# Attention and a gated MLP: the exponentials turned on VectorE in 32x32 blocks, the values as plain fp32 in 32x64 tiles

## The chip, the cores and the metric

One core of one Trainium2 chip runs the whole program. The metric is the device time of an execution in microseconds, the median of several runs.

## What is computed

Eight batches of eight heads, 576 positions, 64 values a head, all in fp32. Rotary attention is followed by an MLP with a spatial gate:

```python
def rotate(x):
    x1, x2 = (x[..., :half], x[..., half:])
    return np.concatenate([x1 * cos - x2 * sin, x1 * sin + x2 * cos], axis=-1)
q_rot, k_rot = (rotate(q), rotate(k))
scores = scale * np.matmul(q_rot, k_rot.transpose(0, 1, 3, 2))
scores = scores - np.max(scores, axis=-1, keepdims=True)
attn = np.exp(scores)
attn = attn / (np.sum(attn, axis=-1, keepdims=True) + 1e-09)
x = np.matmul(attn, v)          # then all heads side by side: (8, 576, 512)
h = np.maximum(x @ w_in, 0.0)   # 512 to 1024
u, v = (h[..., :d_ff // 2], h[..., d_ff // 2:])
v_n = (v - mean(v)) / sqrt(var(v) + 1e-06)
gated = u * (w_spatial @ v_n + b_spatial)
out = gated @ w_out
```

The weights of the MLP come as float64 and are decoded on the chip from their two 32-bit words.

## The kernel before

The unit of attention is a pair of heads; there are 32 pairs, four to a batch. A batch's MLP needs the four pairs of its batch, so it runs in among the attention of the next batch; the last batch's MLP runs alone.

Precision is kept by splitting each fp32 operand into a high and a low part of type fp32r and adding the products high by high, high by low and low by high. A matmul of fp32r is one weight load and one pass; a matmul of plain fp32 is two loads and two passes.

**Preparing a pair** (`prepare`). q and k are loaded transposed, each with a copy whose halves are swapped (two blocks of 576 columns in `st`). GpSimd multiplies both blocks with the tables `tabs` (L452) and adds them (L456); ScalarE and VectorE make the high and low parts; nine transfers on SP's queue stack them into `qs`, `ks` and `qz`, so that high and low parts of a head lie in the two halves of the partitions. Pair 0 alone (`prepare_whole`) keeps plain fp32.

**Scores** (`scores`). Nine chunks of 128 queries to a pair (five of them per head, the two heads' last 64 queries together). A chunk takes four matmuls of 288 columns (six for the joint one, L590; plain fp32 for pair 0, L600), then VectorE takes the maximum (L614) and ScalarE the exponential with its sum (L616). Two buffers `sc` of PSUM hold scores.

**Values** (`values`, pairs 4 to 31). TensorE transposes the exponentials in blocks of 128x128 (L633, 42 a pair), ScalarE copies the result as its high part (L644), VectorE subtracts to make the low part (L357), and TensorE multiplies both with the split V (L657); VectorE adds the two halves of the result (L672). Pairs 0 to 3 (`values_plain`) do the same without a split: transposes (L693), one copy (L700, L702), plain fp32 matmuls into the two 64-column tiles of the array, one per head (L731).

**Normalising** (`normalise`). The inverse sums are turned on VectorE (L765), written to DRAM and read back spread over the partitions (`rt`, `rb`); GpSimd multiplies (L769).

**MLP** (`mlp`). Per batch 360 matmuls in four stages: `pa` (L804, 512 columns), `pb` (L827), `pc` (L845), `pd` (L863), 288 columns each.

**The order** is written out before the program is built: `Program.run` is a planner that plays the instructions through with a cost for each, takes on every engine the ready one with the smallest key, and so fixes each engine's list. Keys are worked out from constants at the top (20 a pair, 80 a batch). Buffers are slots of pools (`SLOTS`); an instruction that needs one waits until it is free. Idle time of TensorE in the first 100 us is filled with matmuls on zeros (`warm`, L937). All loads and stacking transfers go on SP's queue.

Of the kernel before, what the change touches and what calls it, by code (L numbers as in the profile page):

```python
# [9 lines left out]
F32 = mybir.dt.float32  # L10
# [22 lines left out]
TO_PE = 105  # L33
SLOTS = {
    "stage": 3, "lk": 1, "vraw": 2, "vs": 2, "e2": 4, "e1": 2, "eh": 7, "rb": 1, "x32": 1, "xg": 7, "m": 4,
    "small": 3, "nmx": 3, "rt": 2, "sc": 2, "pv": 1, "pm": 3,
}
PSUM = {"sc": 1024, "pv": 512, "pm": 512}
MOE_START, MOE_LENGTH = 92.26, 81.46
DEC_V = [25.09, 132.15, 53.7, 5.9]  # L40
DEC_S = [56.31, 101.35, 34.39]
DEC_U = [50.38, 88.1, 14.23, 96.01]
DEC_ON = 5.18
DEC_O = [146.33, 201.67, 143.69, 195.96]

CHUNKS = [
# [3 lines left out]
]  # L50
CW = 3 * P

PLAIN = 4

WHOLE = 1
Q0 = 3 * TW
CHUNKS2 = [
    ([(0, 0), (1, 0), (0, 1), (1, 1), (0, 2), (1, 2)], [(0, P, 0, 0, 384)]),
    ([(0, 3), (1, 3), (0, 4)], [(0, P, 0, 384, 192)]),
]  # L60
S_AT2 = [[3.49, 4.95, -15.25, -11.82, -19.9, 2.65], [13.02, 24.28, 17.64]]
KT_STEP2 = [2.28, 0.35]
VALUES_AT2 = [-5.73, 46.17]
EARLY = 82.72
STEAL = 87.67
WARM_FROM, WARM_FULL, WARM_TO, WARM_NS, WARM_AFTER, WARM_COLS = 2500, 44958.22, 100000, 170, -0.15, 384
PATIENT = (DVE, ACT, POOL)
UNTIL = -56.22
LATE_LOAD = 2200
S_AT = [-0.24, 4.67, 2.11]  # L70
KT_STEP = 1.19
K_MAX, K_EXP, K_T, K_HI, K_LO, K_AV, K_HALF, K_ADD = 3.66, 16.17, 8.38, -7.48, 1.67, 4.25, 6.99, 12.36
K_LOAD, K_ROPE, K_SUM, K_HIQ, K_LOQ, K_LOK, K_STACK, K_STACK2, K_V, K_VLO = 27, 8, 8, 9, 9, 11, 30, 8, -2, -9
NORM = [-11.45, 57.29, 34.19, 6.63, 21.14]
FIRST = 6
PREP = [30.19, 35.32, -8.17, -24.92, 16.24, 1.9, 50.58, 22.5, 37.15, -9.46]
PREP_E = [54.12, 16.7, 11.17, -20.62, -5.02, 16.96, 39.13, 32.7, -16.4, -6.16]
PREP_AT = [4.76, 4.93, -9.37, 11.39, 24.89, 30.25]
PLAIN_E = [1.95, 2.05, -3.82, 3.33, 11.36]
PLAIN_AT = [-10.96, 10.02, -2.27, -27.43]  # L80
NORM_E = [38.01, -1.87, 12.98, 16.78, -11.57]
MOE0 = [87.11, 88.14]
K_NORM, K_RELU, K_GATE, K_GHI, K_GLO, K_OB, K_OUT = 28.57, -7.71, 10.98, 19.59, 15.51, -9.41, -27.84


def pe_ns(n, m=P):
    return max(m * 5 // 6 + 3, n * 11 // 24)
# [25 lines left out]
class Op:  # L113
    def __init__(self, costs, key, f, new, port, late):
        self.costs, self.key, self.f, self.new, self.port = costs, key, f, new, port
        self.eng, self.late = None, late
        self.waits, self.after, self.bufs = 0, [], []
        self.unknown, self.due = 0, 0


class Program:
# [5 lines left out]
    def op(self, eng, ns, key, f, r=(), w=(), new=(), port=False, late=0):  # L127
        return self.either({eng: ns}, key, lambda e: f(), r, w, new, port, late)

# [22 lines left out]
    def run(self, make, warm):  # L152
# [28 lines left out]
        idle = 0  # L181
        events.append((WARM_FROM, n, "wake", None))
# [3 lines left out]
        while events:  # L186
            now = events[0][0]
            while events and events[0][0] == now:
# [14 lines left out]
                else:  # L203
# [6 lines left out]
                    for a in o.after:  # L210
                        a.waits -= 1
                        if not a.waits:
                            late = TO_PE if PE in a.costs and o.eng != PE else 0
                            heapq.heappush(events, (now + late, n, "ready", a))
                            n += 1
            for e in LATENCY:
                if busy[e]:
                    continue
                passed, chosen = [], None
                while ready[e] and not chosen:  # L220
                    item = heapq.heappop(ready[e])
                    if item[2].eng:
                        continue
# [5 lines left out]
                    else:  # L229
                        passed.append(item)  # L230
                if chosen and e in PATIENT:
                    soon[e] = {a for a in soon[e] if not a.eng and a.due > now}
                    if any(a.key < min(chosen.key, UNTIL) and a.due < now + chosen.costs[e] * 0.5 for a in soon[e]):
# [7 lines left out]
                if e == PE and not chosen and max(WARM_FROM, idle + (WARM_AFTER if now > WARM_FULL else 0)) <= now < WARM_TO and (free["pv"] or free["pm"]):  # L241
                    chosen = warm()
                    pool = "pv" if free["pv"] else "pm"
                    chosen.bufs[0].pool, chosen.bufs[0].slot = pool, free[pool].pop(0)
                    index[chosen] = len(index)
                    left += 1
                if chosen:
                    for b in chosen.new:
                        b.tile = make(b)
# [18 lines left out]
def tile_attention_gated_mlp(  # L268
# [24 lines left out]
    def make(b):  # L293
        tag = f"{b.pool}{b.slot}"
        if b.pool in PSUM:
            return ps.tile([P, PSUM[b.pool]], F32, tag=tag, name=b.name, bufs=1)
        if b.pool == "rt":
            b.scratch = dr.tile([9, P], F32, tag=tag, name=b.name + "d", bufs=1)
# [15 lines left out]
    tabs = T([P, 2 * S], F32, "tabs")  # L314
    ident = T([P, P], F32, "ident")
# [3 lines left out]
    wsp = T([P, 4, 2, S], F32R, "wsp")  # L319
    wt1 = T([P, S], F32R, "wt1")  # L320
    wt2 = T([P, S], F32R, "wt2")
    vn = T([P, 4, 2, HF], F32R, "vn")
    vt1 = T([P, HF], F32R, "vt1")
    vt2 = T([P, HF], F32R, "vt2")

    qs = [T([P, S + TW], F32R, f"qs{a}") for a in range(2)]
    ks = [T([P, TW + S], F32R, f"ks{a}") for a in range(2)]
    qz = T([P, 2 * S], F32R, "qz")
# [4 lines left out]
    def setup():  # L333
        nc.vector.memset(zero, 0.0)
        make_identity(nc, ident)
# [3 lines left out]
        fill(qs[0][:, S:], 0.0)  # L339
        fill(qs[1][:, :TW], 0.0)  # L340
# [688 lines left out]
```

## Time and profile before

| | |
|---|---|
| time, median of 3 runs | 945.76 us (944.73 to 948.39) |
| span of the profiled execution (its own time is not on the page) | 943.9 us |
| instructions in the span | 19676 |
| TensorE matmuls / weight loads | 931.7 us / 857.2 us busy |
| VectorE, ScalarE, GpSimd | 678.2, 745.8, 568.6 us busy |
| mean granted TensorE clock | 0.999 of full speed |

The span runs from the first to the last instruction; the median of the runs is 1.9 us above it. Matmuls overlap one another and their ends are modelled, so TensorE's busy time is not its work: how far apart matmuls start is read from the chain of waits and from the timeline.

### The profile page before, as it was taken

The page shows a single profiled execution, that of the slowest core. Times are in us where ns is not written, and L with a number is a line of the kernel's source. Part 1 is how long each engine was busy: PE and PEld are TensorE (multiplying, and loading weights), DVE is VectorE, ACT ScalarE, POOL GpSimd, SP SyncE. Part 2 cuts the span into 40 slices and gives each one's busy share as a digit, 9 for nine tenths or more (in the row PEclk, how much of TensorE's full clock was granted, in tenths as well). Part 3 has the DMA queues.
Part 4 walks back from the last instruction along what each step waited for, and adds up shares of the span by engine and source line. Part 5 has one row for each costly group of instructions (what it writes and reads, how often), then busy time and mean ns, then how long its engine had stood idle before and what let it go on. Part 6 is the DMA issues. An engine that isn't in the chain of part 4 may idle for free.

```text
span 943.9 us, 19676 instructions
## 1 busy us (share of the span) xinstructions
PE 931.7 (99%) x6714; PEld 857.2 (91%) x6714; DVE 678.2 (72%) x1478; ACT 745.8 (79%) x1839; POOL 568.6 (60%) x500
## 2 busy tenths in 40 slices
PE   8999999999999999999999999999999999999998
PEld 4566799998999989999899999999999998999998
DVE  7998887768866687676877668776786768766331
ACT  4898899778987789787987779877898778977452
POOL 6685677654776557585665657656476665653132
PEclk9999999999999999999999999999999999999999
DMA  8887545455434645445445453536543555430101
GB/s 297 256 241 198 170 114 151 111 161 161 100 107 118 172 128 144 106 120 159 127 113 144 128 140 104 146 108 166 146 103 111 129 160 144 104 67 14 64 1 51
DMA packets 57382, 124.65 MB, mean 132 GB/s; under 512 B 13249, under 2 KB 15169, under 8 KB 57282
## 3 DMA queue, kind: packets, MB, share of 16 engines
q1 hardware_dynamic: 56594, 122.73, 47.4%
q8 instruction: 53, 0.87, 0.4%
q10 hardware_dynamic: 688, 0.66, 0.2%
q14 instruction: 47, 0.39, 0.1%
HBM read 66.03 MB, written 9.58 MB: 80 GB/s over the span
## 4 chain that ended last, share of the span: by engine, by line
PE 75%; ACT 11%; DMA 6%; DVE 3%; POOL 2%; SPq 2%; issue 2%; POOLq 0%; DVEq 0%; ACTq 0%
PE pc L845 13%; PE sc L590 13%; PE pv L657 11%; PE pd L863 11%; PE tp L633 11%; PE pb L827 8%; PE pa L804 5%; ACT e L616 3%; DMA st<-in_qk_dram 3%; ACT eh L644 2%; SPq L351 2%; POOL st L452 1%; PE pv L731 1%; ACT avt L674 1%; DMA ks<-st 1%
## 5 line engine op out<-in xcount | busy, mean ns | idle before, releaser
L357 DVE TENSOR_TENSOR el<-tp,eh 128x384 fp32r<-128x384 f32 x336 | 185.7, 555 | 130.9 <-ACT eh L644 122.6
L644 ACT ACTIVATE eh<-tp 128x384 fp32r<-128x384 f32 (+1 forms) x504 | 217.7, 434 | 65.4 <-PE tp L633 58.1
L616 ACT ACTIVATE e<-sc,nmx 128x576 f32<-128x576 f32 x288 | 213.4, 742 | 49.6 <-DVE nmx L614 46.0
L614 DVE TENSOR_REDUCE nmx<-sc 128x1 f32<-128x576 f32 x288 | 214.4, 749 | 21.8 <-PE sc L590 19.1
L452 POOL TENSOR_TENSOR st<-st,tabs 128x576 f32<-128x576 f32 x122 | 172.0, 1436 | 68.2 <-DMA st<-in_qk_dram 39.2
L633 PE MATMUL tp<-ident,e 128*128 128x128 f32 (+1 forms) x1176 | 197.0, 272 | 0.6 <-DVE eh L357 0.2
L633 PEld LDWEIGHTS tp<-ident,e 128*128 128x128 f32 (+1 forms) x1176 | 146.5, 138 | 12.8 <-DVE el L357 1.8
L657 PE MATMUL pv<-eh,vs 128*128 128x384 f32 (+1 forms) x560 | 147.4, 304 | 0.0
L827 PE MATMUL pb<-x,wi 128*128 128x288 f32 x768 | 146.2, 307 | 0.3
L845 PE MATMUL pc<-wsp,vn 128*128 128x288 f32 x768 | 146.0, 306 | 0.0
L863 PE MATMUL pd<-g,wo 128*128 128x288 f32 x744 | 139.0, 305 | 0.0
L590 PE MATMUL sc<-ks,qs 128*128 128x288 f32 x620 | 135.7, 308 | 3.0 <-ACT e L616 1.3
L804 PE MATMUL pa<-wi,x 128*128 128x512 f32 x448 | 132.6, 406 | 0.0
L590 PE MATMUL sc<-lk,qz 128*128 128x288 f32 x558 | 119.6, 296 | 0.0
L827 PEld LDWEIGHTS pb<-x,wi 128*128 128x128 f32 x768 | 113.3, 189 | 5.2 <-DVE el L357 1.5
L845 PEld LDWEIGHTS pc<-wsp,vn 128*128 128x128 f32 x768 | 113.2, 189 | 1.1
L657 PE MATMUL pv<-el,vs 128*64 128x384 f32 (+1 forms) x448 | 113.8, 295 | 0.0
L863 PEld LDWEIGHTS pd<-g,wo 128*128 128x128 f32 x744 | 109.7, 189 | 2.4 <-PE pc L845 0.4
L590 PEld LDWEIGHTS sc<-ks,qs 128*128 128x128 f32 x620 | 98.1, 189 | 12.4 <-ACT e L616 4.3
L657 PEld LDWEIGHTS pv<-eh,vs 128*128 128x128 f32 x560 | 98.4, 188 | 4.3
L357 POOL TENSOR_TENSOR g<-u,g 128x288 fp32r<-128x288 f32 x64 | 51.8, 819 | 69.7 <-ACT g L354 64.4
L590 PEld LDWEIGHTS sc<-lk,qz 128*128 128x128 f32 x558 | 89.1, 188 | 0.0
(172 smaller groups left out, 1428.5 us busy)
## 6 DMA issues: line engine op xcount, KB each, us to landing
st<-in_qk_dram SPq DMA_DIRECT2D x62, 576.0 KB
ks<-st SPq DMA_DIRECT2D x124, 160.0 KB
qs<-st SPq DMA_DIRECT2D x124, 144.0 KB
vr<-in_v_dram SPq DMA_DIRECT2D x32, 320.0 KB
qz<-st SPq DMA_DIRECT2D x62, 144.0 KB
out_dram<-ob SPq DMA_DIRECT2D x31, 288.0 KB
ws<-in_w_spT_dram SPq DMA_DIRECT2D x2, 576.0 KB
tabs<-in_tab_dram ACTq DMA_DIRECT2D x2, 288.0 KB
```

The costliest lines, as they stand in the source:

```text
L357: eng.tensor_tensor(out=lo, in0=src, in1=hi.bitcast(F32), op=ALU.subtract)
L452: f = lambda e: e.tensor_tensor(out=st[j][:, cols], in0=st[j][:, cols], in1=tabs[:, cols], op=ALU.mult)
L590: nc.tensor.matmul(pt[:, c * 512:c * 512 + HALF], lhsT=lhsT, rhs=rhs[:, k0 + c * HALF:k0 + (c + 1) * HALF], start=(n == 0), stop=(n == len ...
L614: op(DVE, 665, key + k_max, lambda: nc.vector.tensor_reduce(out=nmx.tile, in_=tops(), op=ALU.max, axis=AX.XY, negate=True), r=[pt], w=[nmx ...
L616: op(ACT, 730, key + k_exp, lambda: nc.scalar.activation(e[:, e0:e0 + S].rearrange("p (c n) -> p c n", c=2), tops(), AF.Exp, bias=nmx.tile ...
L633: nc.tensor.transpose(out=tp[:e.shape[1], m * P:m * P + P], in_=e, identity=ident)
L644: nc.scalar.activation(h, p, AF.Copy)
L657: nc.tensor.matmul(pv[0:rows, c1:c2], lhsT=vs[:, kt, h, vp, :], rhs=part[:, c1:c2], start=(kt == 0 and n == 0 and c1 == 0), stop=last)
L804: nc.tensor.matmul(pm.tile, lhsT=lhsT, rhs=win[1, d][:, j, :], start=(d == 0 and n == 0), stop=(d == 3 and n == len(todo) - 1))
L827: nc.tensor.matmul(pm[:, :HALF], lhsT=win[0, d][:, i, f * P:(f + 1) * P], rhs=x[d][:, at:at + HALF], start=(d == 0 and n == 0), stop=(d == ...
L845: nc.tensor.matmul(pm[:, :HALF], lhsT=lhsT, rhs=rhs, start=(t == 0 and n == 0), stop=(t == 4 and n == 1))
L863: nc.tensor.matmul(pm[:, :HALF], lhsT=wout[d,][:, i, m * P:(m + 1) * P], rhs=gs[d][:, at:at + HALF], start=(d == 0 and n == 0), stop=(d == ...
```

## The change

**Exponentials.** A chunk's 128x576 exponentials are turned by one transpose instruction on VectorE, which turns each 32x32 block by itself. So a key of block `kb` lies in partition 32g + k, and the columns hold the 32 queries of row group g of each chunk: 144 per head and row group. The result `tu` has one buffer (a second one, and a second one for V, lie in space that is used later, for pairs 1 and 3).

**Values.** For each of 18 key blocks, eight plain fp32 matmuls of 144 columns: four row groups of 32 partitions (each with its own queries) by two column groups of 64 (the heads). V is loaded four times, once for each row group. The results lie in two buffers `pm` and one of the two score buffers. A pair's values are issued in three portions of six blocks. There are no transposes on TensorE, no high and low parts of exponentials or V, and no additions of halves.

**Pairs 0 to 3** have plain fp32 scores from the rotated q and k, one head in 64 partitions at a time, with no stacking transfers. Pair 0's loads, rotations and sums are issued head by head. For pairs 1 to 3 only one block of q and k is loaded; the swap of halves and the sum are two matmuls, with an identity and with a signed permutation (`ident`), and ScalarE copies the result. The split scores of pairs 4 to 31 keep their form; q gets its columns in an order that suits the transposes.

**Normalising.** For pairs 0 to 4 the inverse sums are put on a diagonal and spread by a matmul with ones; for later pairs they go through DRAM as before. VectorE scales straight from PSUM.

**Loads and order.** The first loads follow a list (`LOADS`). The decoding of a weight loses VectorE steps to ScalarE and GpSimd; the spatial weights are prepared after pair 3. The planner counts TensorE's instruction words and the bytes in transfer; its costs and constants are new. Stages of the MLP wait for all their inputs before their first matmul.

The core of the diff:

```diff
 SLOTS = {
-    "stage": 3, "lk": 1, "vraw": 2, "vs": 2, "e2": 4, "e1": 2, "eh": 7, "rb": 1, "x32": 1, "xg": 7, "m": 4,
-    "small": 3, "nmx": 3, "rt": 2, "sc": 2, "pv": 1, "pm": 3,
+    "stage": 4, "lk": 2, "vraw": 1, "alt_t": 1, "alt_v": 1, "e": 4, "tu": 1, "rb": 1, "xg": 7, "m": 4,
+    "small": 3, "nmx": 3, "rt": 2, "sc": 2, "pm": 4,
 }
...
+LOADS = [
+    "tab0", "st00", "tab1", "st01", "st1", "vr0", "wi10", "wi11", "wi12", "wi13", "st2", "vr1", "wi00", "st3", "vr2", "wi01", "wi02", "st4", "vr3", "wi03", "st5", "vr4",
+]
...
+        def get_v():
+            n = NQ * 2 * D
+            src = v[b, hp]
+            for g in range(4):
+                load(at(vr.tile, 32 * 4 * n * g, (4 * n, 32), (n, 4), (1, n)), at(src, 0, (n, 32), (32 * n, 4), (1, n)))
...
+        def rope_half(j, part, a):
+            rows, cols = slice(64 * a, 64 * a + 64), slice(S * part, S * part + S)
+            f = lambda e: e.tensor_tensor(out=st[j][rows, cols], in0=st[j][rows, cols], in1=tab2[rows, cols], op=ALU.mult)
...
+        def on_pe(j, cols, pt):
+            for n in range(2):
+                nc.tensor.matmul(pt[:, :cols.stop - cols.start], lhsT=ident[:, n], rhs=st[j][:, S * n + cols.start:S * n + cols.stop], start=(n == 0), stop=(n == 1))
...
+        def values(n):
+            outs = [b[:, at:at + Q4] for first in (0, Q4) for b, at in ((pv[0], first), (pv[1], first), (pv[2], first), (pv[2], 512 + first))]
+            for kb in range(NB * n // parts, NB * (n + 1) // parts):
...
+                for a in range(2):
+                    at = (kb + TW // 32 * a) % NB
+                    for g in range(4):
+                        rows = slice(32 * g, 32 * g + 32)
+                        nc.tensor.matmul(outs[g][64 * a:64 * a + 64], lhsT=vr[rows, NQ * (at % 4) + at // 4, a, :], rhs=tu[rows, kb, Q4 * a:Q4 * a + Q4], start=(kb == 0), stop=(kb == NB - 1), tile_position=(32 * g, 64 * a))
...
         def mm():
-            if t < 4:
-                c0 = t * P
-                parts = [(qs[a][:, a * P + c0:a * P + c0 + P], ks[a]), (qz[:, a * (S + TW) + c0:a * (S + TW) + c0 + P], lk.tile)]
+            if kt:
+                pq = (hq, lq)[n_q].bitcast(F32)
+                rows = slice(0, P) if c == 8 else slice(64 * heads[0], 64 * heads[0] + 64)
+                parts = [(jq[:, n_q] if c == 8 else pq[rows, P * (c % 4):P * (c % 4) + P], kt[rows, :S])]
...
+        def turn():
+            src = e.tile.rearrange("p (b n) -> p b n", n=32)
...
+            nc.vector.transpose(out=dst, in_=src)
+
+        op(DVE, dve_ns(S), key + k_turn, turn, r=[e, *[(tu, TILES[0])][:1 - first]], w=[(tu, c)], new=[tu] if first else [])
...
+        def scale():
+            last = pv[2].tile.rearrange("p (g n) -> p g n", g=2)
+            for n in range(2):
+                nc.vector.tensor_tensor(out=x32[:, n], in0=pv[n][:, :Q4], in1=rb[:, n], op=ALU.mult)
+            nc.vector.tensor_tensor(out=x32[:, 2:], in0=last[:, :, :Q4], in1=rb[:, 2:], op=ALU.mult)
```

## Rows read from the trace of the kernel before

**Rows 1.** The page's first part: busy time, share of the span, instructions.

```profile
PE 931.7 (99%) x6714; PEld 857.2 (91%) x6714; DVE 678.2 (72%) x1478; ACT 745.8 (79%) x1839; POOL 568.6 (60%) x500
```

**Rows 2.** Windows: stretch, its length, each engine's busy time (instructions), clock, DMA share, GB/s.

```profile
0.00:100.00 100.00, 93.51 (x611) 58.87 (x611) 88.77 (x148) 76.48 (x180) 64.72 (x69) 1.00 0.84 250
...
450.58:563.12 112.54, 112.38 (x827) 107.20 (x826) 82.62 (x185) 93.26 (x231) 71.99 (x62) 1.00 0.49 131
...
888.00:944.00 56.00, 52.51 (x355) 49.71 (x353) 13.12 (x45) 21.82 (x52) 14.26 (x15) 0.99 0.07 27
```

**Rows 3.** The chain in order of time, steady part and end: start, length, what.

```profile
450.58 0.83 ACT e L616 x2
...
486.18 1.05 PE sc L590 x8
...
563.12 0.83 ACT e L616 x2
...
888.09 11.63 PE pa L804 x50
...
912.77 14.95 PE pc L845 x112
...
937.34 3.19 PE pe L880 x24
```

**Rows 4.** The chain in order of time, the first 100 us.

```profile
0.75 4.36 DMA st<-in_qk_dram
...
20.90 1.12 PE sc L600 x8
...
23.04 1.16 PE sc L600 x4
...
24.68 0.80 PE pv L731 x4
...
59.84 0.82 PE pv L731 x10
```

**Rows 5.** Timeline of TensorE's matmuls around 54 us: start, length, instruction, count.

```profile
53.86 0.54 PE L731 MATMUL pv<-et_3a,vr 128*64 128x384 f32 x1
53.87 0.54 PE L731 MATMUL pv<-et_3b,vr 128*64 128x384 f32 x1
54.23 0.49 PE L731 MATMUL pv<-et_3a,vr 128*64 128x384 f32 x1
```

**Rows 6.** Timeline of TensorE's weight loads in the same stretch.

```profile
53.86 0.13 PEld L731 LDWEIGHTS pv<-et_3a,vr 128*64 128x64 f32 x1 [0.17 <-issue]
53.86 0.13 PEld L731 LDWEIGHTS pv<-et_3b,vr 128*64 128x64 f32 x1
53.91 0.14 PEld L731 LDWEIGHTS pv<-et_3a,vr 128*64 128x64 f32 x1
```

**Rows 7.** Groups of one batch, 450.58 to 563.12: busy us, mean ns, idle before.

```profile
L644 ACT ACTIVATE eh<-tp 128x384 fp32r<-128x384 f32 (+1 forms) x72 | 31.1, 434 | 8.9 <-PE tp L633 8.3
...
L614 DVE TENSOR_REDUCE nmx<-sc 128x1 f32<-128x576 f32 x36 | 26.9, 748 | 2.7 <-PE sc L590 2.4
L616 ACT ACTIVATE e<-sc,nmx 128x576 f32<-128x576 f32 x36 | 26.7, 741 | 5.3 <-DVE nmx L614 5.0
L357 DVE TENSOR_TENSOR el<-tp,eh 128x384 fp32r<-128x384 f32 x48 | 26.6, 555 | 19.3 <-ACT eh L644 18.2 <-PE pv L657 0.2
...
L357 DVE TENSOR_TENSOR eh<-tp,eh 64x256 fp32r<-64x256 f32 (+1 forms) x24 | 8.5, 356 | 3.6 <-ACT eh L644 3.1
...
L672 DVE TENSOR_TENSOR x<-pv,avt 64x384 f32<-64x384 f32 (+3 forms) x20 | 7.5, 388 | 2.0 <-ACT avt L674 1.8
...
L765 DVE STREAM_TRANSPOSE rt<-sums 128x32 f32<-128x32 f32 x4 | 0.8, 206 | 0.1
```

**Rows 8.** DMA queues: packets, MB, share of the 16 engines' span.

```profile
q1 hardware_dynamic: 56594, 122.73, 47.4%
q8 instruction: 53, 0.87, 0.4%
```

More of the change, by code (lines that the diff above doesn't have):

```diff
@@ L222, in run @@
                     if item[2].eng:
+                        continue
+                    if kept and any(b.pools[0] in PSUM for b in item[2].new):
+                        passed.append(item)
+                        continue
+                    if e == DMA and item[2].kb in (512, 576) and moved > now + FULL:
+                        passed.append(item)
+                        heapq.heappush(events, (moved - FULL, n, "wake", None))
+                        n += 1
                         continue
@@ new lines, in low_q @@
+        def low_q(a):
+            own, other = half(a)
+            load(raw(qs[other, a, :]), raw(lq[own]))
+        for a in range(2):
+            late = K_LATE * a
+            prog.move(2, 288, key - K_STACK + late, lambda a=a: high_k(a), r=[(st[1], 1)], w=[("ks", a)])
+            prog.move(2 + a, 325, key - K_STACK + late, lambda a=a: high_q(a), r=["hq"], w=[("qs", a, 0), ("qz", a)])
+            prog.move(1, 164, key - K_STACK2 + late, lambda a=a: low_q(a), r=["lq"], w=[("qs", a, 1)])
@@ L574, in scores @@
[L574 to L587 removed]
+        key = 20 * i
@@ new lines, in attention @@
+        for n in range(parts):
+            fill = FILL if i < FILL_PAIRS and n < parts - 1 else 0
+            o = op(PE, NB * 243 // parts + 330 + 243 * (i < SPREAD and n == parts - 1) + fill * 165, key + K_VAL + K_CHUNK * n, lambda n=n: values(n), r=[vr, *[(tu, c) for c in TILES], *(spared if i in ALT else []), *([(rb, "m")] if i < SPREAD and n == parts - 1 else [])], w=[*pv, *[("go", i)][:1 - n]], new=pv if n == 0 else [])
+            o.words = NB * 32 // parts + 2 * fill + 32 * (i < SPREAD and n == parts - 1)
@@ L602, in tops @@
-        def tops():
-            return pt.tile.rearrange("p (c n) -> p c n", c=2)[:, :, :HALF]
-        heads = [a] if t < 4 else [0, 1]
-        need = [lk] + [("qs", h, j) for h in heads for j in range(2)] + [("ks", h, j) for h in heads for j in range(2)] + [("qz", h) for h in heads]
-        if i < WHOLE:
-            q, kf = lk
-            need = [(kf, 0), (kf, 1), (q, 0) if t == 0 else (q, 1), *([(q, 0)] if t else [])]
-            if t == 0 and a == 0:
-                op(PE, 4 * pe_ns(HALF), key, lambda: mm_whole((0,)), r=[(kf, 0), (q, 0)], w=[pt], new=[pt])
@@ L741, in normalise @@
-    def normalise(i, sm, x32, key):
-        K_INV, K_GET, K_X, K_XHI, K_XLO = NORM_E if i < NP else NORM
+                for n_c in range(2):
+                    nc.tensor.matmul(pt[:, n_c * 512:n_c * 512 + HALF], lhsT=lhsT, rhs=rhs[:, n_c * HALF:n_c * HALF + HALF], start=(n == 0), stop=(n == len(parts) - 1))
+        if kt:
+            need = [("hq", "lq")[n_q], *([(t, a) for a in heads for t in ("hq0",)] + [(kt, 0, a) for a in heads] if i == 0 else [("jq", i)][:i in QPE] + ([(kt, 0, 0), (kt, 0, 1)] if i in KPE else [(kt, 0)]))]
+        else:
+            need = [lk, *[t for a in heads for t in (("qs", a, 0), ("qs", a, 1), ("ks", a), ("qz", a))]]
@@ new lines, in scores, with flat, invert @@
+        op(DVE, dve_ns(S), key + k_turn, turn, r=[e, *[(tu, TILES[0])][:1 - first]], w=[(tu, c)], new=[tu] if first else [])
+    def flat(rb):
+        return rb.tile.rearrange("p g n -> p (g n)")
+    def invert(i, sm, key):
+        need = [("sums", i % 2, c) for c in range(9)]
+        key += (NORM_E if i < FIRST else NORM)[0]
+        op(ACT, 100, key, lambda: nc.scalar.activation(sm[:, 0:9], sm[:, 0:9], AF.Copy, bias=1e-9), w=need)
+        op(DVE, 130, key, lambda: nc.vector.reciprocal(out=sm[:, 0:9], in_=sm[:, 0:9]), w=need)
@@ new lines, in normalise @@
+        if i < SPREAD:
+            op(ACT, 650, key + K_X, copy, r=pv, w=[rb, (rb, "m")])
+        else:
+            invert(i, sm, key)
+            op(DVE, 125, key + K_INV, lambda: nc.vector.transpose(out=rt.tile, in_=sm), r=need, w=[rt], new=[rt])
+            prog.move(1, 16, key + K_INV, put, r=[rt], w=[(rt, 1)], late=300)
+            prog.move(3, 320, key + K_GET, get, r=[(rt, 1)], w=[rb], new=[rb], late=300)
+        op(DVE, dve_ns(S) + 220, key + K_X, scale, r=pv, w=[rb])
+        op(ACT, 660, key + K_XHI, high, r=[x32, *([("gated", i // NP - 1)] if i >= NP and i % NP == NP - 1 else [])], w=[(x, 0)], new=[x])
```

750 lines of the change are left out of this document (385 added, 365 removed), and 3 rows, old and new, of the table CHUNKS.

## The prediction

> **What bounds the kernel now.** I read the shares of the span first: TensorE is busy for 99% of it, in 6714 matmuls and as many weight loads [rows 1]. A busy TensorE need not be at its peak, because ends are modelled, so the second view is the windows: one batch period of 112.5 us has TensorE busy for 112.4 us, with 827 matmuls, VectorE 82.6 and ScalarE 93.3 at full clock; the first 100 us are different (VectorE 88.8, DMA share 0.84, TensorE 93.5 with warming matmuls in it) [rows 2]. The third view is the chain in order of time. The same ScalarE instruction stands at 450.58 and 563.12, so a batch takes 112.54 us; and from 888.09 to 940.53 the chain is nothing but the last batch's MLP back to back, 52.4 us, for instance 112 matmuls of 288 columns in 14.95 us (133 ns each) [rows 3]. There is no other engine in that stretch: the matmuls are at TensorE's pace.
>
> So a steady batch is 52.4 us of MLP and 60.1 us of four pairs, 15.0 us a pair. The scores of a pair are 38 matmuls of 288 columns at 131 ns (eight in 1.05 us [rows 3]), 5.0 us. The other 10.0 us are the 42 transposes and the 36 matmuls of high and low parts with V. That is what the change replaces.
>
> **The change part by part.**
>
> *Values in 32x64 tiles.* All transposes leave TensorE, and so do the split matmuls. In their place a pair has 18 key blocks, each with four row groups by two heads: eight plain fp32 matmuls of 144 columns, each of which is two loads and two passes (so the plain values show in the trace: two passes for one matmul, a second one at +0.37 us [rows 5]). If the eight tiles run side by side, a key block costs two passes. What a pass costs I take from the plain values of pairs 0 to 3. At 384 columns passes start 0.37 us apart [rows 5]; at 192 columns a tile a stretch of two key blocks, two passes each, took 0.82 us, 0.205 a pass [rows 4] (twelve matmuls in the two tiles, of which the chain lists ten). That is a slope of 0.86 ns a column and a fixed 40 ns. For 144 columns: 0.164 us with the fixed part, 0.124 without. A pair's values then cost 18 x 2 x 0.164 = 5.9 us or 18 x 2 x 0.124 = 4.5 us. I take 5.2, between the two, since with eight tiles one tile's fixed part can lie beside another's columns, at least in part; both ends stay in the range. The fixed ends of the three portions in which a pair's values are issued are in it (24.68: two pairs of passes took 0.80 us where two starts 0.37 us apart make 0.74, so some 0.06 us per change of shape [rows 4]).
>
> Do tiles run side by side? Two column tiles do: et_3a and et_3b start their passes 10 ns apart, and their first weight loads start in the same hundredth, the second ones 50 ns later [rows 5, 6]. Two row groups do as well: eight passes of 64x64 tiles with 288 columns took 1.12 us, 140 ns each, while four passes of the undivided form took 1.16 us, 290 ns each [rows 4]. Four row groups at once no row shows.
>
> *The sum for TensorE.* MLP 8 x 52.4 = 419.5 us. Split scores of 28 pairs 140 us. Values of 32 pairs 32 x 5.2 = 166 us. Scores of pairs 0 to 3, now plain and one head after the other, 36 chunks of four passes at 1.16 us [rows 4], and I take 41 us in all (35 without the fixed part). Rotation sums of pairs 1 to 3 as matmuls with an identity and a permutation: 1152 columns for q and k, two matrices, two passes, 4.0 us and 16 fixed parts of 0.04, so 4.6 a pair and 14 in all. Together 780.5 us.
>
> *What is not covered.* At the start the first rows must land (4.4 us for the first load, from 0.75 [rows 4]), and behind them stand a rotation, a sum and a scaling, now in halves by head; GpSimd first fills more constants. I take 12 us until TensorE has real work, as an estimate (7 to 16). In the first batch VectorE has 36 maxima and 36 transposes at 0.75 us, 54 us, and decodes weights between them, beside 76 us of TensorE work: 8 us idle (0 to 20). At the end 3.4 us, as now (940.53 to 943.9). In the steady part I add 6 us, under 1%: the kernel before loses 0.1% there [rows 2], but the new order has one buffer for the turned exponentials and holds a score buffer for the values.
>
> *VectorE.* Per batch 26.6 us of low parts, 8.5 of the last ones and 7.5 of additions go, 42.6 us [rows 7]. What comes is 36 transposes of 128x576. The trace has only one of 128x32, at 206 ns; the maximum over the same 576 columns takes 748 ns [rows 7]. The lower bound is 206, the upper 900; I take 750, since the columns must be passed through as they are for the maximum: 27 us. The scaling from PSUM adds three instructions of about 0.39 us a pair [rows 7], 4.7 us. VectorE then has 82.6 - 42.6 + 27 + 4.7 = 72 us in a batch of some 94: it is not the bound, and even 900 ns would make it 77.
>
> *ScalarE* loses 31.1 us of copies a batch [rows 7] and gains little: about 62 us, hidden under TensorE. *GpSimd* loses the low parts of V and the multiplication by the inverse sums; hidden as before. If TensorE were faster still, VectorE would be next.
>
> *Transfers.* V is loaded four times over, so 0.96 MB more a pair, 31 MB. Now 122.7 MB take 47.4% of the queues' time [rows 8], 3.65 us a MB; 31 MB add 113 us, and 560 us in 812 is 69%. On SP's queue the four V loads stand ahead of the stacked q and k of later pairs; a load comes a pair ahead, so I cost it at nothing in the steady part. Without that cover it is the 4 us of such a load per batch. The weights of the later stages move behind the first pairs' loads, and their decoding loses two VectorE steps; that is in the 8 us.
>
> *Sum.* 780.5 + 12 + 8 + 6 + 3.4 = 809.9 us of span. The page gives the profiled execution only its span of 943.9, 1.9 us under the median of the runs; with that, 812 us.
>
> **The rivals.**
>
> *Instructions do not come fast enough.* A key block is 32 instructions in 0.29 us, 9 ns each. The densest stretch of this kind in the trace is those 12 matmuls in 0.82 us, 68 ns each [rows 4], though passes start as little as 10 ns apart [rows 5]. With 25 ns for each of the 16 passes of a block a pair's values take 18 x 0.4 = 7.2 us, 2.0 more, and the kernel 812 + 64 = 876 us. Instructions come in packets: 53 for 13,428 instructions [rows 1, 8], 253 each. A steady pair will need 832 instructions (576 for the values, 76 for the scores, 180 for its share of the MLP), 3.3 packets in 23 us, where now it is 1.7 in 28; it becomes the bound when a packet takes over 7 us. One packet's transfer is 0.4% x 16 x 943.9 / 53 = 1.1 us [rows 8], which speaks against it. The Trainium skill has a rule that speaks against the change: "TensorE: Matmul & The Clock Gate", section "Wait — 56ns, not 53.3ns?", says that matmuls start no closer than about 25 ns however few their columns, and some 62 ns where the sequencer decodes them in software. By that rule, as an estimate, the kernel would take 876 us with 25 ns and some 1,220 us with 62; the two starts 10 ns apart [rows 5] do not agree with it, but they are two and not a stream.
>
> *The pairs' own chain becomes the bound.* The turned exponentials have one buffer, the values need all nine chunks, and while they run one of the two score buffers is theirs. A chunk with one score buffer takes 0.53 (scores [rows 3]) + 0.75 (maximum) + 0.74 (exponential) [rows 7] and some 0.25 of hand-over, 2.25 us; nine and the values make 25.5 us, against 52.4/4 + 5.0 + 5.2 = 23.3 us of TensorE work. That costs 2.2 x 28 = 62 us: 874 us. For it speaks that so little is buffered; against it that four exponentials may be ready ahead and that both score buffers are free most of the time.
>
> *Slower: the row groups take turns.* If the four row groups of a key block run one after another, the values take 4 x 5.2 = 20.8 us a pair and the kernel 812 + 32 x 15.6 = 1311 us; two at a time, 10.4 us and 978 us. It decides from 9.4 us a pair on (134 us of gain over 32 pairs). Against it stand the 64-row tiles [rows 4]; four groups no row shows. Here the skill's "TensorEngine Tiling (Array Packing)", "Key Properties", is on the change's side about tiles in parallel, but adds that a change of tiling mode drains the engine; the 0.06 us above is what a row shows of that.
>
> **How the numbers follow.** The forecast's case, eight tiles side by side and TensorE the bound, 0.70; within it 772 (values at 4.5 us, no idle time in the first batch) to 845 us (values at 5.9, stalls of 2%). Too few instructions 0.08, the pairs' chain 0.12, row groups in turn 0.10. The range 770 to 885 takes in all but the last and the edges. A measurement can tell about 0.5% (the runs shown lie within 0.4%): faster 0.89, same 0.01, slower 0.10.
>
> **What would show it.** A steady batch of 92 to 96 us with TensorE busy throughout; a last MLP of 52 us as now; a portion of six key blocks taking 1.5 to 2.0 us; 128x576 transposes on VectorE of about 0.75 us; DMA share near 0.7. The forecast is wrong if a portion takes 2.4 us (instructions) or 6 us (row groups in turn), or if TensorE's rows show idle time ended by VectorE or ScalarE in every pair (the chain).

## The result and the profile after

The changed kernel takes 892.96 us (median; 891.51 to 894.87) against 945.4 us for the kernel before (944.73 to 948.39): the ratio is 0.942, with a 95% interval of 0.937 to 0.947. It is faster, as forecast, but by 5.8% and not by 14%. The profiled execution has a span of 889.7 us where the forecast's sum had 809.9, so 80 us are to be found. Every time here and below is the median of a kernel's runs, without those over 1.5% above its fastest.

The page's first part for the changed kernel, which answers to [rows 1], two of its groups (busy us, mean ns, idle before), and its DMA queues, which answer to [rows 8]:

```profile
PE 858.7 (97%) x13709; PEld 757.9 (85%) x13709; DVE 580.6 (65%) x1169; ACT 497.5 (56%) x1239; POOL 511.2 (57%) x509
...
q1 hardware_dynamic: 98962, 148.12, 71.6%
q8 instruction: 108, 1.77, 0.9%
...
L771 DVE STREAM_TRANSPOSE tu<-e 128x576 f32<-128x576 f32 x288 | 216.5, 762 | 17.7 <-ACT e L761 9.7
...
L715 PE MATMUL pv<-tu,vr 32*64 32x144 f32 x9216 | 177.4, 288 | 11.2 <-issue 11.2
```

The reader sees four terms of the forecast in place: TensorE is still the busiest engine, the turn of 128x576 values takes 762 ns (750 taken), the transfers have 71.6% of the queues (69%), and VectorE and ScalarE fell well below TensorE. Twice as many instruction packets arrive (108 for 53).

Where the time lies, by stage: the windows from the first scores to the first MLP (13.70 to 126.80), then to the second MLP, a steady batch, and the last MLP. They answer to [rows 2]; the columns are the same.

```profile
13.70:126.80 113.10, 108.32 (x1614) 73.19 (x1614) 89.37 (x141) 68.01 (x162) 80.16 (x77) 0.95 0.76 190
126.80:243.80 117.00, 106.78 (x1890) 96.63 (x1888) 82.37 (x162) 69.42 (x175) 82.21 (x74) 0.99 0.76 174
345.90:446.40 100.50, 97.56 (x1667) 89.13 (x1666) 67.72 (x140) 58.65 (x148) 60.09 (x58) 1.00 0.83 189
832.00:889.70 57.70, 53.88 (x362) 50.98 (x360) 12.37 (x45) 21.82 (x52) 14.09 (x16) 0.99 0.07 27
```

Three readings. A steady batch is 100 us (99.5 as the mean of the four from 345.9 to 744.0), against 112.5 before and 92 to 96 forecast. The last MLP costs about what it did (TensorE is busy for 53.9 us, 52.5 before [rows 2]). And the first MLP begins at 126.8 us, where the kernel before began it at 97.7 and the forecast had it at 12 + 76 + 8 = 96: the start gives away 29 us of what the batches win. The line of the kernel before:

```profile
97.73 0.96 PE L804 MATMUL pa<-wi,x 128*128 128x512 f32 x3
```

TensorE's timeline shows the values themselves and what interrupts them (start, length, instruction, count; in brackets the idle time before it):

```profile
109.47 1.78 PE L715 MATMUL pv<-tu,vr 32*64 32x144 f32 x96
111.18 0.39 PE L1009 MATMUL warm<-zero 128*128 128x256 bf16 x2
111.50 0.96 PE L715 MATMUL pv<-tu,vr 32*64 32x144 f32 x39
114.16 1.22 PE L715 MATMUL pv<-tu,vr 32*64 32x144 f32 x57 [1.71 <-issue]
```

A portion of 96 passes takes 1.71 us from its first start to the start of the next matmul of another shape, 17.8 ns a pass with the way out of the small tiles in it. Eight passes then take 0.142 us, about what one alone was taken to cost (0.124 to 0.164), so all eight tiles run side by side: 18 key blocks make 5.1 us a pair (5.2 forecast). The next portion stands still for 1.71 us after 39 passes, and nothing that the profile shows is waited for: the instructions are not there yet. All of TensorE's waits in the changed kernel, longest sums first (us, times, longest):

```profile
PE pv L715 <- issue: 11.2, 13, 1.7
PE sc L750 <- DVE rb L826: 5.5, 7, 1.2
PE sc L750 <- ACT e L761: 4.6, 6, 2.3
PE sc L750 <- ACT sums L781: 1.5, 1, 1.5
```

The second row is the scaling that gives back the score buffer which the values hold; the kernel before had no wait of this kind.

### The profile page after: what moved, and what is told of

It reads as the page before. It is cut to its first block, busy times and chain, and to the rows that moved or that the text cites. A ratio compares the mean times of both kernels' runs of the same rounds, so it can differ in the third digit from the quotient of the medians.

```text
span 889.7 us, 32677 instructions
## 1 busy us (share of the span) xinstructions
PE 858.7 (97%) x13709; PEld 757.9 (85%) x13709; DVE 580.6 (65%) x1169; ACT 497.5 (56%) x1239; POOL 511.2 (57%) x509
## 3 DMA queue, kind: packets, MB, share of 16 engines
q1 hardware_dynamic: 98962, 148.12, 71.6%
## 4 chain that ended last, share of the span: by engine, by line
PE 65%; DMA 11%; issue 9%; SPq 4%; DVE 4%; POOL 4%; ACT 2%; POOLq 0%; DVEq 0%; ACTq 0%
PE sc L750 15%; PE pv L715 11%; PE pc L915 11%; PE pb L897 9%; PE pa L874 7%; PE pd L935 5%; DMA st<-in_qk_dram 4%; PE warm L1009 4%; SPq L429 3%; DMA ks<-st 2%; POOL st L563 2%; PE pr L616 1%; DMA vr<-in_v_dram 1%; DVE tu L771 1%; DVE nmx L760 1%
## 5 line engine op out<-in xcount | busy, mean ns | idle before, releaser
L771 DVE STREAM_TRANSPOSE tu<-e 128x576 f32<-128x576 f32 x288 | 216.5, 762 | 17.7 <-ACT e L761 9.7
L563 POOL TENSOR_TENSOR st<-st,tab 128x576 f32<-128x576 f32 x112 | 157.8, 1429 | 58.2 <-DMA st<-in_qk_dram 43.5
L715 PE MATMUL pv<-tu,vr 32*64 32x144 f32 x9216 | 177.4, 288 | 11.2 <-issue 11.2
L715 PEld LDWEIGHTS pv<-tu,vr 32*64 32x64 f32 x9216 | 147.9, 131 | 35.8 <-issue 31.8
L897 PE MATMUL pb<-x,wi 128*128 128x288 f32 x768 | 117.5, 297 | 0.9 <-ACT vv L973 0.8
L935 PE MATMUL pd<-g,wo 128*128 128x288 f32 x744 | 113.6, 297 | 0.0
L435 POOL TENSOR_TENSOR vn<-vv,vn 128x512 fp32r<-128x512 f32 (+1 forms) x40 | 51.4, 1292 | 98.9 <-ACT vn L432 98.6
L435 POOL TENSOR_TENSOR x<-rb,x 128x64 fp32r<-128x64 f32 (+1 forms) x96 | 59.4, 652 | 79.9 <-ACT x L432 79.9
L874 PEld LDWEIGHTS pa<-wi,x 128*128 128x128 f32 x448 | 79.1, 188 | 14.7 <-issue 1.8
L578 POOL TENSOR_TENSOR st<-st 128x576 f32<-128x576 f32 x56 | 80.0, 1429 | 2.9
```

The costliest lines, as they stand in the source:

```text
L435: eng.tensor_tensor(out=lo, in0=src, in1=hi.bitcast(F32), op=ALU.subtract)
L563: f = lambda e: e.tensor_tensor(out=st[j][:, cols], in0=st[j][:, cols], in1=tab2[:, cols], op=ALU.mult)
L578: f = lambda e: e.tensor_tensor(out=st[j][:, :S], in0=st[j][:, :S], in1=st[j][:, S:2 * S], op=ALU.add)
L715: nc.tensor.matmul(outs[g][64 * a:64 * a + 64], lhsT=vr[rows, NQ * (at % 4) + at // 4, a, :], rhs=tu[rows, kb, Q4 * a:Q4 * a + Q4], start= ...
L771: nc.vector.transpose(out=dst, in_=src)
L874: nc.tensor.matmul(pm[:, :HF], lhsT=lhsT, rhs=win[1, d][:, j, :], start=(d == 0 and n == 0), stop=(d == 3 and n == len(todo) - 1))
```

## The experiments

Two theories for the steady part: the change of array shape at a portion's edges costs more than the 0.06 us taken (A), or TensorE runs out of instructions, from their own pace (B) or behind the fourfold V (F). For the start: VectorE's list with its weight decodings (C), the transfers (D), the chain over one score buffer (E), or TensorE's own list with its matmuls of zeros (G). The start is that of the first MLP in the profile, 126.8 us in the changed kernel. The changed kernel was not run again beside the experiments; the kernel before was, each time, and took 944.9 to 945.5 us.

**Shape, once a portion.** A matmul of zeros with the whole array, 16 columns, in the middle of each portion; and the control with the same matmul at the edges.

```diff
+ a == 0 and kb == NB * n // parts + 3 and nc.tensor.matmul(pv[1][:, 0:16], lhsT=zero[:, :P], rhs=zero[:, 0:16], start=False, stop=False)
```

> Each of the 96 portions of the values is broken once, after half of its key blocks, by one matmul of zeros of the whole 128x128 array with 16 columns, added into the first columns of the same buffer; everything else stands in the same order. Theory A (a change of array shape costs about 0.35 us there and back, and this is the largest part of the gap in the steady batches): about 96 x 0.35 = 34 us more than the changed kernel, 920 to 930. Rival (a change costs what the forecast took, 0.06 us, and the gaps at the portions are waits for something else): 96 x 0.12 = 12 us or less, 895 to 905.

> The same 96 matmuls of zeros, but each at the edge of a portion (last of the first two, first of the third), where the shape changes anyway: the control for e1_break. Both theories: 96 x (16 columns and one weight load, 0.03 to 0.08 us), 2 to 8 us above the changed kernel, 894 to 901. If it costs as much as e1_break, the matmul itself is the cost and not the shape.

Measured 907.1 us and 895.5: the break costs 14 us over the changed kernel and 11.6 over its control, 0.12 to 0.15 us each, nearer the rival than theory A. The timeline of the run with breaks, around one:

```profile
488.71 0.82 PE L897 MATMUL pb<-x,wi 128*128 128x288 f32 x5
489.46 1.04 PE L715 MATMUL pv<-tu,vr 32*64 32x144 f32 x48
490.44 0.18 PE L712 MATMUL pv<-zero 128*128 128x16 bf16 x1
490.55 1.04 PE L715 MATMUL pv<-tu,vr 32*64 32x144 f32 x48
491.52 0.66 PE L897 MATMUL pb<-x,wi 128*128 128x288 f32 x3
```

From its first pass to the next MLP matmul the broken portion takes 2.06 us (489.46 to 491.52), the unbroken one above 1.71: 0.35 us for the break. So locally it costs what theory A has, and over twice what reached the end: the waits for instructions fell from 11.2 to 5.3 us, and in the start idle time takes some. The rows give the price of a portion, too: half of one, 48 passes, takes 0.98 us to the next start, the whole 1.71, so a pass is 15.2 ns and 0.25 us are independent of their number. And the way in: five MLP matmuls, which make 0.66 us at 133 ns, take 0.75 before the first pass, 0.09 more.

**Shape, five times a portion.**

```diff
+ a == 0 and kb > NB * n // parts and nc.tensor.matmul(pv[1][:, 0:16], lhsT=zero[:, :P], rhs=zero[:, 0:16], start=False, stop=False)
```

> The break of e1_break, but before every key block of a portion except the first: 5 in each of the 96 portions, 480 in all, 384 more than in e1_break. If a change of shape there and back costs 0.31 us and nothing is returned: 480 x 0.31 = 149 us above the changed kernel, less at most the 16 us of stalls for instructions: 1025 to 1045. If the cost that reaches the end is 0.12 to 0.15 us: 950 to 965.

992.4 us: 99.5 more for 480 breaks, 0.21 each, between the two expectations. A steady batch has 60 of them and rises from 99.5 to 113.9 us, 0.24 each. A steady batch's window and a wait of this run:

```profile
375.60:490.10 114.50, 114.31 (x1727) 93.82 (x1726) 67.81 (x140) 58.60 (x148) 59.64 (x58) 1.00 0.71 166
...
PE pv L715 <- issue: 0.6, 2, 0.4
```

With the stream this much thinner the waits for instructions are gone (0.6 us). Their 11 us are returned against the breaks, so a change there and back costs about (99.5 + 11) / 480 = 0.23 us net, the zeros included, which the control puts at 0.03 (2.6 us for 96). It is a lower bound, since other small gaps close as well: the mean granted clock of this run is 1.00 (0.992 in the changed kernel).

**One portion of 288 passes** (576 instructions with their weight loads), from the seventh pair on.

```diff
-CHUNKS = [3, 3]
+CHUNKS = [3, 1]
```

> From the seventh pair on the values come in one portion instead of three: 26 x 2 = 52 changes there and back fewer. Theory A: 52 x 0.35 = 18 us less, 873 to 880, if the longer bursts of short instructions bring no more stalls; theory B (the stalls in which TensorE waits for nothing recorded come from running out of instructions in a burst): a burst of 576 instructions in 5.1 us runs out in every pair, 26 x 1 to 2 us more, so that the two together give 890 to 910. Rival (shape is cheap, no stalls): within 3 us of the changed kernel.

981.6 us, slower than the kernel before. Fewer changes of shape win nothing beside this; TensorE's timeline of one burst, the windows of its two parts, and TensorE's waits:

```profile
439.46 2.67 PE L715 MATMUL pv<-tu,vr 32*64 32x144 f32 x149
444.24 3.89 PE L715 MATMUL pv<-tu,vr 32*64 32x144 f32 x128 [2.11 <-issue]
...
439.46:442.13 2.67, 2.67 (x150) 2.41 (x150) 0.17 (x1) 1.23 (x4) 2.48 (x3) 1.00 1.00 236
444.24:448.13 3.89, 3.89 (x128) 3.47 (x128) 0.00 (x0) 0.00 (x0) 3.13 (x3) 0.56 0.80 191
...
PE pv L715 <- issue: 54.8, 35, 2.6
PE sc L750 <- DVE rb L826: 23.6, 16, 3.3
```

A burst runs for 149 passes, stands for 2.1 us, and goes on at 30 ns a pass, at a granted clock of 0.56: 17.8 / 0.56 makes 32, so this slow pace is the clock's. Theory B's waits are of the size written, 55 us, 44 more than in the changed kernel (26 to 52); the total is not. Another 24 us are waits for the score buffer, which the values then hold longer (5.5 in the changed kernel), and the mean granted clock is 0.972 (0.992). (The order of the list changes with the portions, so part of the 89 us can be order.)

**A quarter of V**, from the seventh pair on, and for all pairs (each quarter is used four times over, so the output is made from part of V).

```diff
-load(at(vr.tile, ..., (n, 4), (1, n)), at(src, 0, (n, 32), (32 * n, 4), (1, n)))
+load(at(vr.tile, ..., (n, 1), (1, n)), at(src, 0, (n, 32), (32 * n, 1), (1, n)))
```

> From the seventh pair on only a quarter of each of the four copies of V is loaded, and used four times over: 26 pairs x 0.96 MB = 25 MB less, same instructions in the same order. Theory F (the stalls in which TensorE waits for instructions come from the fetch queueing behind the fourfold V): stalls in the values fall from 16 to under 6 us and a steady batch from 99.5 to 97 or less; total 873 to 882. Rival (the transfers of V are hidden, the supply of instructions has a pace of its own): steady batches within 0.5 us, total 889 to 896.

> As the kernel with a quarter of V from the seventh pair on, but for all pairs: 6 x 0.96 MB less before the first MLP and in the first batch after it. Theory D (transfers limit the start): the first MLP starts 10 to 20 us before 126.8 and the total is that much below the run with the quarter from the seventh pair on. Theory E or C: start within 3 us of 126.8.

892.3 and 890.0 us; starts 128.3 and 127.3; steady batches 100.1 and 99.7. The DMA share of a steady batch falls from 0.83 to 0.63 and the waits for instructions stay (13.1 and 9.8 us for 11.2). The fourfold V is hidden, and the fetch does not queue behind it: theories D and F fall.

**V cut the other way.**

```diff
-for g in range(4): load(at(vr.tile, 32 * 4 * n * g, (4 * n, 32), (n, 4), (1, n)), at(src, 0, (n, 32), (32 * n, 4), (1, n)))
+for c in range(4): load(at(vr.tile, n * c, (4 * n, 128), (1, n)), at(src, 32 * n * c, (0, 4), (n, 32), (1, n)))
```

> The four transfers of V of each pair are cut the other way: each fills all 128 partitions with a quarter of every partition's bytes, instead of 32 partitions whole. Bytes, number of transfers and every other instruction are the same. Theory D (the stretch before the first MLP is limited by the transfers, which move 205 to 217 GB/s there where the kernel before moved 320 to 420, because a transfer that fills few partitions is slow): the busy share of the transfers falls, the first MLP starts 10 us or more before 126.8, the total is 875 to 885. Rival (the transfers are not what the pairs wait for, or the partitions do not matter): start within 2 us of 126.8, total 890 to 896.

1107.6 us, the largest miss. The transfers' busy share by slices of 3.25 us from 0 to 130, with GB/s, of this run:

```profile
DMA  3999222224527479247955972299674862442245
GB/s 95 215 209 206 76 99 103 101 102 131 150 106 202 128 231 280 115 141 205 359 203 138 282 275 55 101 202 238 154 192 127 170 173 74 129 116 102 95 95 110
...
PE pv L715 <- DMA vr<-in_v_dram: 85.5, 38, 5.1
```

While V moves, a share of 0.2 carries 100 GB/s: with a source that repeats its rows four times the transfers keep some three of the 16 engines at work on the mean, and last. The run says nothing on theory D, but it shows what the cover of V's loads is worth: without it TensorE waits 85.5 us for V.

**Four edits in the start, each with a new order.** The list is planned from costs, so these runs change the order too.

```diff
# e4_late_u
-U_AFTER, O_AFTER = [1, 1, 2, 2], [3, 3, 3, 3]
+U_AFTER, O_AFTER = [3, 3, 3, 3], [3, 3, 3, 3]
# e5_rot_vec
-KPE, QPE = TURNED, TURNED
+KPE, QPE = [], []
# e8_no_v_early
+vr = prepped[0][1] if 1 <= i <= 4 else vr
# e10_no_u_decode
+op(POOL, 1100, key, blank, r=[t0, t1, *after], w=[n], port=True); return
```

> The four decodings of the U half of the input weights wait for the fourth pair's first values instead of the second's and third's: 16 operations of 0.6 us and the products leave VectorE's and GpSimd's list before the first MLP. Theory C (before the first MLP VectorE is what the pairs wait for: 83 per cent busy from 51 to 75 us): the first MLP starts 6 to 10 us earlier than at 126.8, and 3 to 8 us of it reach the end: 885 to 890. Rival (the pairs' chain or the transfers set this stretch): the start moves by under 2 us and the end is the same or later, since the MLP's second product then waits for the late weights: 892 to 900.

> The sums of the rotations of pairs two to four go back from TensorE to VectorE and GpSimd: TensorE loses 48 matmuls of 17 us before the first MLP, VectorE or GpSimd gain 6 sums of 0.7 or 1.4 us. If TensorE sets that stretch (it is busy with matmuls of zeros for 40 us of it, so by the trace it does not): start 10 us earlier. If VectorE and GpSimd set it: start 5 to 8 us later, total 897 to 901. If the transfers set it: within 3 us of the changed kernel.

> Pairs two to five take the V of the first pair, whose loads they leave out (the output of these pairs is made from the wrong V): 4 x 1.28 MB of the 24.6 MB that move in the first 130 us are gone. Theory D (transfers limit the start): at 210 GB/s up to 24 us of transfer go; the first MLP starts 10 to 20 us earlier, total 873 to 883. Rival (a chain over VectorE and the score buffers limits it): start within 4 us of 126.8, total 887 to 895.

> The decoding of the U half of the input weights is left out (zeros stand in their place, so the output is wrong); its four loads stay. VectorE loses 16 operations of 0.6 to 0.7 us and ScalarE 12, all before the first MLP. Theory C (the pairs wait in VectorE's list behind these: four decodings stand among the waits at 76 to 82 and 96 to 102 us): the first MLP starts 8 to 15 us earlier than 126.8, total 878 to 886. Rival (transfers): start within 4 us, total 888 to 895.

922.7, 922.3, 906.9 and 899.1 us; starts 131.6, 140.2, 124.2 and 125.0. (The second also leaves out the exchange of the two halves in the rotation.) Each edit made the kernel slower, mostly between the first and second MLP (143.9, 131.9, 136.2 and 120.8 us for 117.0). What the edits gain and what the new orders cost can't be told apart: no start came more than 3 us earlier, and the whole rose by 6 to 30 us. The next runs keep the order.

**VectorE's work shortened in the same order.**

```diff
# f1_half_max
-in_=tops(pt), op=ALU.max
+in_=tops(pt)[:, :1 + (i >= 4)], op=ALU.max
# f2_short_u: the U weights' operations over W = 128 of 512 columns
```

> The maxima of the first four pairs are taken over half the columns (their exponentials are then shifted by another number): 36 operations of VectorE become about 0.35 us shorter, the order of all lists is unchanged. Theory E (before the first MLP the pace is a chain: one of the two score buffers is held by the values, so scores, maximum, exponential and the next scores follow each other): up to 36 x 0.35 = 13 us, the first MLP starts 6 to 13 us before 126.8, total 880 to 887. If the transfers set the stretch: start within 2 us, total 890 to 896.

> Only a quarter of the columns of the U half of the weights is decoded and used (all four blocks of the first product take the first block's weights); same instructions in the same order: 16 operations of VectorE and 12 of ScalarE become about 0.4 us shorter. Theory C (decodings in front of maxima and turns hold the pairs up at 76 to 82 and 96 to 102 us): start 4 to 7 us before 126.8, total 883 to 889. Theory E or the transfers: start within 2 us, total 890 to 895.

894.5 and 888.6 us; the start of the first is 127.9, that of the second is not known. Theory E's 6 to 13 us did not come. The second lies inside theory C's total (883 to 889), 4.3 us under the changed kernel, and its mean granted clock is 0.996 (0.992); whether its start moved is not shown.

**The matmuls of zeros** after the first 98: 16 columns, every second, none, and none with the shorter maxima; same order.

```diff
-f = lambda e: nc.tensor.matmul(b.tile[:, :WARM_COLS], lhsT=zero[:, :P], rhs=zero, start=True, stop=True)
+f = lambda e: warmed.append(0) or len(warmed) < 99 and nc.tensor.matmul(...)   # g3
```

> The matmuls of zeros that fill TensorE's list after the first 98 (before the first scores) have 16 columns instead of 256; same instructions in the same order. Theory G (TensorE's list, these included, sets the stretch before the first MLP: 78 us of work, 17.5 us of them, 17.6 us of waits after 13.7 us): they take 0.03 to 0.06 instead of 0.104 us, the first MLP starts 7 to 12 us before 126.8 if the granted clock stays, total 881 to 886. Rival (a chain over VectorE and the score buffers sets it): start within 3 us, total 889 to 896. If the clock falls for the lack of work, the plain scores take twice as long and the start comes later than 126.8.

> After the first 98 every second matmul of zeros is left out, 89 of 179, all else in the same order. Theory G: 89 x 0.104 = 9 us, start 5 to 9 us earlier, total 884 to 888. Rival (chain): start within 3 us. Clock falls: start later.

> After the first 98 all matmuls of zeros are left out, all else in the same order. Theory G without a loss of clock: 17.5 us less, of which waits take back some: start 8 to 15 us earlier, total 878 to 885. Rival (chain): waits take all of it back, start within 3 us. Clock falls: the scores and rotations of the stretch, 60 us, run partly at half the clock, start 5 to 30 us later, total 897 to 920.

> As the kernel without these matmuls of zeros, and with the maxima of the first four pairs over half the columns (0.35 us less in 36 operations). If the chain over VectorE is the limit once TensorE's list is shorter: 5 to 13 us earlier than without them alone. If TensorE's list or its clock is still the limit: within 2 us of it.

908.0, 895.8, 905.3 and 898.3 us; starts 137.9, 134.4, 136.8 and 133.1. The windows from 13.7 to 51 us of the changed kernel and of the run without them:

```profile
13.70:51.00 37.30, 36.78 (x170) 23.37 (x170) 30.72 (x44) 22.49 (x54) 26.98 (x22) 1.00 0.88 235
...
13.70:51.00 37.30, 34.31 (x95) 19.64 (x93) 25.91 (x37) 19.54 (x47) 23.96 (x20) 0.77 0.84 219
```

The granted clock falls from 1.00 to 0.77, and the start comes 10 us later. So they do fill TensorE's list, some 17 us of it after 13.7, but they pay for themselves: theory G in its simple form falls. With the clock down, the shorter maxima do help (3.7 us of start, 7 us in all).

**All of it shortened at once:** f1, f2 and the quarter of V for all pairs, same order, zeros as they were.

> The maxima of the first four pairs over half the columns, a quarter of the U weights decoded, and a quarter of V loaded for all pairs, together; same instructions in the same order, matmuls of zeros as in the changed kernel. Theory G (TensorE's own list sets the stretch before the first MLP): start still 122 to 128, total 882 to 891. If the limit only moved from engine to engine in the single runs: start 8 to 20 us earlier, total 870 to 882.

880.9 us, inside the second expectation, with a start of 119.7 between the two. The chain of the changed kernel at that place, in order of time:

```profile
80.75 0.54 DVE vlwi L477
81.29 0.69 DVE tu L771
81.98 0.41 DVE rb L825 x2
82.39 0.38 DVE rb L826
...
82.80 1.90 PE sc L750 x4
84.70 1.40 PE warm L1009 x6
86.09 2.21 PE sc L750 x4
...
89.06 2.22 PE sc L750 x4
91.28 1.40 PE warm L1009 x6
92.67 0.43 PE pv L715
```

The same place with all of it shortened:

```profile
80.91 1.17 PE sc L750 x4
82.08 0.76 PE warm L1009 x6
82.83 1.17 PE sc L750 x4
...
86.36 1.71 PE pv L715 x96
```

The window from 80 to 92 us, first of the changed kernel, then of this run:

```profile
80.00:92.00 12.00, 10.31 (x30) 5.12 (x29) 6.99 (x15) 4.46 (x12) 10.54 (x11) 0.64 0.99 209
...
80.00:92.00 12.00, 12.00 (x232) 7.83 (x230) 7.51 (x18) 6.27 (x18) 8.08 (x11) 1.00 0.65 152
```

In the changed kernel the scaling of the second pair stands on VectorE behind the last steps of two weight decodings, a split (`lk`) and a turn; the score buffer comes free 2 us late, TensorE stands for 1.7 of them, and from then on it runs at the lower of its two clocks: three score tiles of 1.16 us take 1.9 and 2.2, and the zeros, too, take twice as long. By the next portion this is 6.3 us (92.67 for 86.36).

That is not yet the price of the low clock in the start. The control with zeros at the portions' edges leaves all of VectorE's work in place and has the same wait. The timeline there, first of the changed kernel, then of the control, with the control's window:

```profile
82.80 1.90 PE L750 MATMUL sc<-st,lq 64*128 64x288 f32 x4 [1.19 <-DVE rb L826]
...
84.01 1.23 PE L750 MATMUL sc<-st,lq 64*128 64x288 f32 x4 [1.19 <-DVE rb L826]
...
89.46 1.78 PE L715 MATMUL pv<-tu,vr 32*64 32x144 f32 x96
...
80.00:92.00 12.00, 10.66 (x200) 6.96 (x183) 10.48 (x19) 7.17 (x19) 10.02 (x11) 1.00 1.01 215
```

There the clock stays at 1.00. From the end of the wait to the next portion it takes 5.5 us (84.01 to 89.46), in the changed kernel 9.9: the low clock costs 4.4 us here, and the control's first MLP starts at 123.9, 2.9 us earlier (125.5 in the run with one break a portion, which has the same wait and 1.00, too). So of the 7.1 us by which the start moved with all of it shortened, some 3 are the clock's and the rest is the shortened work's, or not assigned. Why the clock fell behind the wait in one run and not in the other no run shows. Single starts that differ by 3 us or less are no evidence for a theory, then: with the maxima shortened, and with a quarter of V, this low spell is there too.

## Why the forecast was too low

**The work was right.** Taking for each shape of matmul the spacing of its starts in an undisturbed stretch (17.8 ns for a pass of the values) times its count, TensorE has, as an estimate, some 787 us of work (780.5 forecast). Values side by side, the price of a turn, the transfers' share, the last MLP, VectorE and ScalarE no bound: each as forecast. The first rival's mechanism is there, but its price was not: a portion runs at 17.8 ns a pass, not 25. The Trainium skill, "TensorE: Matmul & The Clock Gate", section "Wait — 56ns, not 53.3ns?", has starts no closer than about 25 ns; over 96 passes in eight tiles this trace disagrees (1.71 us). The row groups do not take turns. That the values came out at 5.2 us a pair is luck in part: the forecast has 36 x 0.144 us with 0.06 a portion for the edges in it, and the rows above have 288 x 15.2 ns = 4.4 us and three portions of 0.25 + 0.09, 5.4 us. A pass of eight tiles was too dear (0.122 us, the forecast's lower bound of 0.124) and an edge too cheap. (The range's low case does not follow from its terms: 0.7 us a pair and the 8 us off 812 make 782, not 772.)

**What failed is "What is not covered"**, 29 us of idle time that became some 103 (889.7 - 787).

*The first batch, "8 us idle (0 to 20)" and "12 us until TensorE has real work".* Real work begins at 13.7 us, and from there to 126.8 TensorE has 78 us of work, 17.5 of zeros and 17.6 of waits and half clock: 49 us uncovered for the 20 forecast. I had compared VectorE's 54 us with TensorE's 76 as sums, and left out that the lists are served in order and that one score buffer is held by the values. Shown are the half-clock spell at 82 us, worth some 3 us of the start, and that the zeros can't be taken out. The other 26 us are not assigned: with one kind of work shortened at a time the total moved by 1.5 us up to 4.3 down, with all of it by 12, and a version with another order that keeps TensorE fed was not tried. Why the start is late stays open, then.

*The steady part, "I add 6 us".* From 126.8 to 832 us the uncovered time is 50 us, some 17 of it, as an estimate, before the second MLP. The portions' edges: 0.34 us each, where "0.06 us per change of shape" was read from two pairs of passes of one tile shape. Of this, 0.25 stands in the 17.8 ns a pass and so in the 787; in the 50 are 84 x 0.09 = 8 us. The Trainium skill, "TensorEngine Tiling (Array Packing)", section "Key Properties", says that a change of mode drains the engine; the breaks agree, 0.23 to 0.35 us there and back. Instructions that come late, in this stretch: 9 us. Waits for the score buffer (scaling, exponential, sums): 10 us. After one of these, 2.35 us long at 182 us, some 26 matmuls run at the low clock, 3 us. That is 30 of the 50; the rest is in gaps too small for a row, and not assigned.

**The pairs' chain**, a rival with 0.12, came true in small: 10 us after the first MLP, not 62, where the MLP's matmuls stand between; before it, where there are none, it is part of the 49.

The forecast's own check, a batch of 92 to 96 us, failed by 3.5 to 7.5 us (99.5).

## What to carry to other kernels

Where many small tiles replace a few large matmuls, count three prices beside the passes: each change of shape there and back (0.23 to 0.35 us here), the length of a burst that the instruction supply can feed (96 passes at a time cost 11 us of waits in all, 288 at a time 55), and the buffer that the accumulating tiles hold. Ask of the start, where no other work covers a wait, not whether each engine's sum fits but what stands ahead in its list; a wait of 2 us cost 4 more there when the clock fell behind it, and nothing more in a run where it did not. Before a cause is read off one run's rows, look for another run that has the same wait. To test a cause in a planned order, shrink the work and keep the order: four runs that let the order change told almost nothing.

## What the runs showed of the hardware

In eight 32x64 tiles 96 passes of 144 columns took 1.71 us with the way out, 17.8 ns each; a whole-array matmul of 16 columns between them cost 0.35 us there, 0.23 net. In one burst TensorE stood after 149 passes for 2.1 us, waiting for nothing recorded; fewer bytes on the queues did not change such waits (13.1 and 9.8 us for 11.2), a thinner stream did (0.6). Transfers of 320 KB with a source repeated four times moved 100 GB/s at a busy share of 0.2, and TensorE waited 85.5 us for them. After idle times of 1.7 us in three pieces and of 2.35 us the next matmuls took nearly twice their time, for some 10 us at 82 us and some 4 at 182, at granted clocks of 0.64 (80 to 92) and 0.80 (184 to 188); in another run the same wait of 1.19 us was followed by 1.00.
